# A third down product as seven block products, and LayerNorm statistics of twelve tiles moved to ScalarE

## Chip, cores and metric

One core of a Trainium2 chip. The metric is the device time of one execution in microseconds (us), median of several. Every run is profiled, so each run also has its own span and its own mean granted TensorE clock.

## The reference, cut to what matters

Two layers, each a linear-attention block and a gated bilinear block, on 2048 rows of 1024 bf16 elements. The inner width of the bilinear block is 3584.

```python
x = x + _A_ref(_layernorm(x), A_wqkv, A_wo)               # layer one, attention
x = x + _B_ref(_layernorm(x), B_w_gate, B_w_up, B_w_down) # layer one, bilinear
x = x + _A_ref(_layernorm(x), A_wqkv, A_wo)               # layer two
x = x + _B_ref(_layernorm(x), B_w_gate, B_w_up, B_w_down)
# _B_ref: h = (x @ w_gate) * (x @ w_up);  return h @ w_down
```

## The kernel before

A helper records every operation with what it reads and writes, derives the waits, and emits one instruction stream per engine. So an engine works strictly in the order of the program, and a line of a profile is often a helper's line.

Each bilinear block runs in two passes of 1024 rows: gate/up, then down. A down pass is one two-by-two block multiplication with seven products instead of eight, in the order 1, 2, 6, 7, 4, 5, 3. A *plain* product is 56 matmuls with 512 moving columns. Some products are split once more into seven *block products*, 98 matmuls with 256 columns, 7/8 of the columns. The price of that is VectorE's: eight operand sums S1 to S4 and T1 to T4 of 128x1792 elements, and for product three twelve accumulations of 256 columns out of PSUM.

```python
L2DOWN = {(False, 0): "45", (False, 1): "5", (True, 0): "45", (True, 1): "453"}   # (layer two, pass): products split again
...
def run_l2(q, evac):                                   # a product as seven block products
    ...
    order = ((f, 0), (f, 1), (m2, 0), (m6, 0), (m2, 1), (m6, 1), (m7, 0), (m3, 0), (m7, 1), (m3, 1), (m4, 0), (m4, 1))
    for st_, (fn, r) in enumerate(order):
        fn(r)                                          # one or two block products and their accumulations
        ...
        l2_ops(q, "abcdefghijkm"[st_])                 # operand sums scheduled behind this step
```

The LayerNorm of the next block is spread under the down products (`dticks1`): statistics (two passes of `bn_stats` on VectorE), reciprocal deviation on GpSimd, normalisation, then a DMA transpose. At the start of the kernel there is a second form of the statistics, with two accumulating passes on ScalarE:

```python
def ln_s1(i, dst, r_dst):     # ScalarE: sum of x/D; GpSimd: negate it
    P.add("act", lambda e: e.activation(dst, x_res[:, i, :], AF.Copy, scale=1.0 / D, accum_out=mv[j][:, 0:1]), ...)
def ln_s2(i, j, dst, r_dst):  # ScalarE: sum of (x - mean)^2
    P.add("act", lambda e: e.activation(dst, x_res[:, i, :], AF.Square, bias=mv[j][:, 5:6], scale=1.0, accum_out=mv[j][:, 6:7]), ...)
```

Of the kernel before, what the change touches and what calls it, by code (L numbers as in the profile page):

```python
# [180 lines left out]
def build_kernel(nc, A_x, A_wqkv, A_wo, B_w_gate, B_w_up, B_w_down, out):  # L181
# [21 lines left out]
    ORDER0 = "D3A' P1A P7B' P6A D2B' 51 D4B' D3B' R0 56 D2A P1B T0 P7A 57 P5A W P6B T1 D4A R0 P5B S5+"  # L203
    ORDER1 = "P5A' 47' T0 P7B' D4A' P5B' 11 D3A' R0 51 16 D4B' D2B' P1A 17 T1 56 D3B' P6A P1B 41 R0 57 S5+ S2+ D2A P6B 46 P7A"
    ORDER2 = "11 57' D2B' P7B' 16 T0 P5A' 21 D4B' P1A 17 S2+ D3A' P5B' 26 R0 P6A D2A S5+ 41 27 P1B D3B' 46 51 T1 P7A 47 P6B 56 D4A R0"
    L2DOWN = {(False, 0): "45", (False, 1): "5", (True, 0): "45", (True, 1): "453"}
    DSCHED = {
        "45": {"20": "S1:5 S1:4", "21": "S2:5 S2:4", "22": "S3:5 S4:4", "23": "S4:5", "70": "S3:4 T1:4", "72": "T2:4 T3:4", "73": "T1:5",
               "4d": "T4:4", "4j": "T2:5", "4m": "T3:5", "5d": "T4:5"},
        "5": {"20": "S1:5", "21": "S2:5", "22": "S3:5", "23": "S4:5", "41": "T1:5", "42": "T2:5", "43": "T3:5", "5d": "T4:5"},  # L210
        "453": {"20": "S1:5 S1:4", "21": "S2:5 S2:4", "22": "S3:5 S4:4", "23": "S4:5", "70": "S3:4 T1:4", "71": "S1:3", "72": "T2:4 T3:4", "73": "T1:5",
                "4d": "T4:4", "4f": "S2:3", "4j": "T2:5", "4m": "T3:5", "5d": "T4:5 S4:3", "5h": "T1:3", "5k": "S3:3", "5m": "T2:3", "3d": "T3:3", "3f": "T4:3"},
    }
# [110 lines left out]
    with ExitStack() as es:  # L324
# [13 lines left out]
        def vh(o, n):  # L338
            return ah[:, o // 2: o // 2 + n]
# [156 lines left out]
        class LN:  # L496
# [13 lines left out]
            def dst(self, n):  # L510
# [2 lines left out]
                o = (O_XN + [O_WQ])[n % 3] if self.to == "B" and n < 14 else O_XN[n % 2]  # L513
                return vh(o, D), R(o, D * 2)

            def start(self, i):
                assert i == self.n
                if self.to == "A0" and i in LN_ACT:
                    j = ln_s1(self.order[i], *self.dst(i))
                    self.q_s.append((i, j))  # L520
                else:
                    j = ln_a(self.order[i])
                self.n += 1
                self.q_b.append((i, j))

            def s2(self, upto=NST):
                while self.q_s and self.q_s[0][0] <= upto:
                    i, j = self.q_s.pop(0)
                    ln_s2(self.order[i], j, *self.dst(i))

            def b1_one(self):
                if self.q_b:
# [816 lines left out]
        def layer_B(lnp, nxt, first):  # L1349
# [301 lines left out]
            def down(ps_, ticks, tail):  # L1651
# [30 lines left out]
                def flat(o):  # L1682
                    return vh(o, 1792).rearrange("p (j c) -> p j c", c=256), R(o, 3584)

                def xbuf(i, half=ps_):
                    c0 = 1024 * half + 256 * i
                    return xnT[:, 0:7, c0:c0 + 256], _seg(O_XT, 7, S * 2, c0 * 2, (c0 + 256) * 2)

                tr, ha_ = [flat(O_T + 3584 * i) for i in range(3)], [flat(O_HA + 3584 * i) for i in range(4)]
                sbuf2 = {"4": [xbuf(i) for i in range(3)], "5": tr if "4" in l2d else [xbuf(1 + i) for i in range(3)], "3": [xbuf(i, 1 - ps_) for i in range(3)]}  # L1690
                tbuf2 = {"4": [flat(RE), flat(RE + 3584), flat(O_XN[0])], "5": [xbuf(3) if "4" in l2d else ha_[2], ha_[0], ha_[1]], "3": [ha_[2], ha_[3], xbuf(3, 1 - ps_)]}
                r4 = [(vf(o, 512), R(o, 2048)) for o in (RC, RC + 2048, RB + 28672, RB + 30720)]
                l2w = {}
                for q in l2d:
# [17 lines left out]
                def run_l2(q, evac):  # L1712
                    W = l2w[q]
                    DB, UB = (B_DX, B_DV[:2]) if q == "4" else (B_DV, B_DX[:2] if q == "5" else B_DX[2:])
                    need = {5: ("S1", "T1"), 6: ("S2", "T2"), 7: ("S3", "T3"), 4: ("T4",), 3: ("S4",), 1: (), 2: ()}

                    def mm(i, r, bank, half, start=False):
                        (a, ra), (b, rb) = W["mm"][i]
                        assert all(n in W["done"] for n in need[i]), (q, i, W["done"])
                        P.add("pe", lambda e: [e.matmul(psb(bank)[:, 256 * half:256 * half + 256], a[:, k, 128 * r:128 * r + 128], b[:, k, :],  # L1720
                                                        start=(start and k == 0), stop=(k == 6), skip_group_check=True) for k in range(7)],
                              rd=ra + rb, pwr=[bank])

                    def hf(ap, h):
                        return ap[:, 256 * h:256 * h + 256]

                    def acc(t, h, r, uh, src):
                        d, rd_ = rout[t]
                        sv, rs = src[t]
                        stt(hf(d, h), hf(psb(UB[r]), uh), CD, hf(sv, h), rs, rd_, prd=[UB[r]])  # L1730

                    def put(t, r):
                        P.add("act", lambda e: e.copy(hf(psb(DB[t]), 0), hf(psb(UB[r]), 1)), prd=[UB[r]], pwr=[DB[t]])

                    def put5(t, r):
                        P.add("dve", lambda e: e.tensor_tensor(out=hf(psb(DB[t]), 1), in0=hf(psb(UB[r]), 1), in1=hf(r4[r][0], 0), op=ALU.add),
                              prd=[UB[r]], rd=r4[r][1], pwr=[DB[t]])

                    if q == "3":
                        rin = rout = [(rtmp[4 + t], rr(4 + t)) for t in range(4)]  # L1740
                    else:
                        rin, rout = [xq(1, 0, t) for t in range(4)], r4

                    def first_(r):
                        mm(5, r, UB[r], 0, True)
                        mm(1, r, UB[r], 1)
                        if q == "5":
                            P.add("act", lambda e: e.copy(hf(r4[r][0], 0), hf(psb(UB[r]), 0)), prd=[UB[r]], wr=r4[r][1])
                            put(r, r)
                        else:  # L1750
                            acc(r, 1, r, 0, rin)
                            acc(r + 2, 1, r, 0, rin)
                            acc(r, 0, r, 1, rin)

                    def m6(r):
                        mm(6, r, UB[r], 1)
                        if q == "5":
                            put5(r, r)
                        else:
                            acc(r, 1, r, 1, rout)  # L1760

                    def m7(r):
                        mm(7, r, UB[r], 1)
                        if q == "5":
                            put5(r + 2, r)
                            put(r + 2, r)
                        else:
                            acc(r + 2, 1, r, 1, rout)
                            acc(r + 2, 0, r, 1, rin)

                    def m2(r):
                        mm(2, r, DB[r], 0)

                    def m3(r):
                        mm(3, r, DB[r], 1)
                        evac(r)

                    def m4(r):
                        mm(4, r, DB[r + 2], 0)
                        evac(r + 2)  # L1780
                    f = first_
                    order = ((f, 0), (f, 1), (m2, 0), (m6, 0), (m2, 1), (m6, 1), (m7, 0), (m3, 0), (m7, 1), (m3, 1), (m4, 0), (m4, 1))
                    for st_, (fn, r) in enumerate(order):
                        fn(r)
                        if st_ == 9:
                            ring_issue()
                            ring_issue()
                        l2_ops(q, "abcdefghijkm"[st_])

                tail(0)  # L1790
                for qi, q in enumerate(DPROD):
# [106 lines left out]
            def dticks1(q, t):  # L1898
                if is_last:
                    return  # L1900
                if q != "3":
                    nxt.step_t(1)
                    nxt.b2_one()
                    nxt.b1_one()
                    if t % 2 == 0 and nxt.n < 8:
                        nxt.start(nxt.n)
                if q == "1" and t == 3:
                    for c in (1, 2, 4):
                        tw_load("k", c)
                if q == "7" and t == 3:  # L1910
                    for c in (2, 4):
                        tw_load("q", c)
                if q == "5":
                    s_make(nxt.order, 0)[t]()
                if q == "5" and t == 3:
                    for w in "kq":
                        load_w(w, 0)
                        t, v, c0, base = WSRC[w]
                        dma(t[:, 4:8, 512:1024], v[:, 4:8, c0 + 512:c0 + 1024], _seg(base + 4 * D * 2, 4, D * 2, 1024, 2048), KW[w][1])
                        tw_load(w, 3)  # L1920
                    tw_load("q", 1)
                if q == "3":
                    stash(12 + t)
                    nxt.step_t(1)
                    nxt.b2_one()
                    nxt.b1_one()
                    nxt.start(8 + t)
                    if t == 3:
                        for k in range(4):
                            stash(8 + k)  # L1930
# [77 lines left out]
```

## Time and profile before

| | before |
|---|---|
| median of the first three runs | 1436.43 us (1435.66 to 1438.34) |
| products five and three of layer one's second down pass | 22.78 us (707.96 to 730.74) |
| start of product five to layer two's first gate/up pass | 239.96 us (to 947.92) |
| from there to the end of product five of layer two's first down pass | 230.31 us (to 1178.23) |

The two later marks, and what lies between them, are these lines of the same view (start, duration, what):

```profile
947.92 7.77 PE ps L1385 x36
...
1117.09 7.15 DMA arena<-arena
1124.34 0.55 DVE arena L492
1124.88 0.61 DVE arena L453
...
1160.43 17.75 PE ps L1720 x161
1178.23 10.74 PE ps L1802 x49
```

### The profile page before, as it was taken

How to read it: one execution, taken by the hardware profiler on the slowest of the kernel's cores; microseconds unless marked ns; L12 is line 12 of the kernel's file. 1: busy time of each engine (PE TensorE's matmuls, PEld its weight loads, DVE VectorE, ACT ScalarE, POOL GpSimd, SP SyncE). 2: the span in 40 equal slices, each digit the busy share in tenths (PEclk: the TensorE clock that was granted, in tenths of full speed). 3: DMA queues.
4: the chain of work that ended last, by engine and by line, in shares of the span. 5: the costliest groups of instructions: out<-in, count | busy, mean ns of one | idle time of the engine just before them, and what ended most of it. 6: DMA issues, size and time to landing. Idle time of an engine off the chain costs nothing.

```text
span 1433.9 us, 21771 instructions
## 1 busy us (share of the span) xinstructions
PE 1420.6 (99%) x8107; PEld 786.8 (55%) x8167; DVE 1209.5 (84%) x2370; ACT 688.2 (48%) x1408; POOL 149.9 (10%) x181
## 2 busy tenths in 40 slices
PE   9999999999999999999999999999999999999999
PEld 4444444555546566664544444446766475666547
DVE  6897878999988799988679978778888887888888
ACT  5882355444410266652157813667776004767400
POOL 2203621000010000002000045310000100000000
PEclk9999999999999999999999999999999999999999
DMA  7868978997786777768993266767775976777653
GB/s 227 203 144 234 219 173 199 300 303 266 255 266 211 235 256 255 244 235 300 232 286 96 89 171 165 182 181 254 262 243 194 288 256 226 261 258 259 205 192 120
DMA packets 272586, 320.73 MB, mean 224 GB/s; under 512 B 164064, under 2 KB 215008, under 8 KB 272480
## 3 DMA queue, kind: packets, MB, share of 16 engines
q1 hardware_dynamic: 272480, 319.34, 73.1%
q8 instruction: 64, 1.05, 0.3%
q14 instruction: 42, 0.34, 0.1%
HBM read 236.45 MB, written 73.40 MB: 216 GB/s over the span
## 4 chain that ended last, share of the span: by engine, by line
PE 84%; DVE 8%; ACT 2%; DMA 2%; issue 2%; POOL 1%; SPq 1%; POOLq 0%; DVEq 0%; ACTq 0%
PE ps L1385 28%; PE ps L1466 17%; PE ps L1802 14%; PE ps L1201 8%; PE ps L960 6%; PE ps L1720 5%; PE ps L1303 4%; DVE arena L798 3%; PE ps L928 2%; DMA arena<-arena 1%; DVE arena L453 1%; DVE arena L801 1%; DMA arena<-in_A_wqkv_dram 1%; ACT arena L658 1%; SPq L426 1%
## 5 line engine op out<-in xcount | busy, mean ns | idle before, releaser
L798 DVE TENSOR_TENSOR arena<-arena 128x512 f16<-128x512 f16 (+9 forms) x1019 | 498.8, 517 | 60.1 <-ACT arena L1470 34.2
L1385 PE MATMUL ps<-arena 128*128 128x512 f16 x1888 | 457.0, 379 | 1.0 <-DVE arena L801 0.9
L801 DVE SCALAR_TENSOR_TENSOR arena<-ps,arena 128x512 f16<-128x512 f32 (+3 forms) x545 | 353.8, 663 | 68.5 <-PE ps L1802 28.4
L1466 PE MATMUL ps<-arena 128*128 128x256 f16 x2184 | 287.5, 273 | 1.0 <-DVE ps L1479 1.0
L1385 PEld LDWEIGHTS ps<-arena 128*128 128x128 f16 (+1 forms) x1888 | 182.9, 98 | 163.4 <-ACT ps L1414 3.8
L1466 PEld LDWEIGHTS ps<-arena 128*128 128x128 f16 (+1 forms) x2184 | 212.2, 98 | 91.5 <-ACT arena L1470 6.9
L1802 PE MATMUL ps<-arena 128*128 128x512 bf16 (+1 forms) x1102 | 242.6, 379 | 0.9
L1802 PEld LDWEIGHTS ps<-arena 128*128 128x128 f16 x1120 | 109.5, 98 | 130.4 <-DVE arena L798 0.4
L1390 ACT ACTIVATE arena<-ps 128x512 f32<-128x512 f32 x224 | 133.8, 597 | 76.4 <-PE ps L1385 61.6
L1470 ACT ACTIVATE arena<-ps 128x256 f32<-128x256 f32 x351 | 125.1, 384 | 26.9 <-PE ps L1466 22.0
L960 PE MATMUL ps<-arena 128*128 128x512 f16 (+1 forms) x606 | 134.1, 379 | 1.0 <-ACT arena L967 0.4
L1201 PE MATMUL ps<-arena 128*128 128x512 bf16 x498 | 114.7, 379 | 0.7
L1303 PE MATMUL ps<-arena 128*128 128x512 bf16 x502 | 110.3, 379 | 0.5
L456 POOL TENSOR_SCALAR arena<-arena 128x1 f32<-128x1 f32 x59 | 20.8, 353 | 806.8 <-DVE arena L455 806.8
L1476 ACT COPY ps<-ps 128x256 f32<-128x256 f32 x182 | 66.3, 364 | 74.6 <-DVE arena L801 28.3
L960 PEld LDWEIGHTS ps<-arena 128*128 128x128 f16 x616 | 59.5, 98 | 74.7 <-ACT arena L967 5.8
L1414 ACT COPY ps<-ps 128x512 f32<-128x512 f32 x112 | 65.4, 584 | 64.3 <-PE ps L1385 52.1
L1062 POOL TENSOR_TENSOR arena<-arena 128x1024 f16<-128x1024 f32 x32 | 78.2, 2445 | 154.6 <-DVE arena L1060 146.3
L1720 PE MATMUL ps<-arena 128*128 128x256 f16 (+1 forms) x784 | 86.8, 273 | 0.7 <-DVE arena L801 0.5
L453 DVE BATCH_NORM_STATS2 arena<-arena 128x6 f32<-128x512 bf16 x118 | 81.3, 689 | 5.4 <-DMA arena<-in_A_x_dram 3.3
L1479 DVE TENSOR_TENSOR ps<-ps,arena 128x256 f32<-128x256 f32 x182 | 76.6, 427 | 10.5 <-PE ps L1466 9.5
L1303 PEld LDWEIGHTS ps<-arena 128*128 128x128 f16 x512 | 50.1, 98 | 60.4
(70 smaller groups left out, 939.8 us busy)
## 6 DMA issues: line engine op xcount, KB each, us to landing
arena<-w_scratch SPq DMA_DIRECT2D x84, 896.0 KB, 4.6
arena<-t_scratch SPq DMA_DIRECT2D x32, 896.0 KB, 6.1
arena<-in_B_w_down_dram SPq DMA_DIRECT2D x24, 896.0 KB, 5.7
arena<-sp_scratch SPq DMA_DIRECT2D x26, 768.0 KB, 4.2
w_scratch<-arena SPq DMA_DIRECT2D x28, 512.0 KB, 6.3
arena<-w_scratch SPq DMA_DIRECT2D x28, 384.0 KB, 4.8
x_scratch<-arena SPq DMA_DIRECT2D x40, 256.0 KB, 7.7
arena<-x_scratch SPq DMA_DIRECT2D x40, 256.0 KB, 5.6
```

The lines of the kernel that those rows point to most:

```text
L453: P.add("dve", (lambda h: lambda e: e.bn_stats(st[j][:, 6 * h:6 * h + 6], x_res[:, i, (D // 2) * h:(D // 2) * (h + 1)]))(h), rd=r_x(i, (D ...
L798: P.add("dve", lambda e: e.tensor_tensor(out=out, in0=a, in1=b, op=op), rd=rd, wr=wr, prd=prd)
L801: P.add("dve", lambda e: e.scalar_tensor_tensor(out=out, in0=a, scalar=sc, in1=b, op0=ALU.mult, op1=op1), rd=rd, wr=wr, prd=prd)
L960: P.add("pe", lambda e: [e.matmul(psb(bank), a[0][:, k, :], b[0][:, k, :], start=(q in (1, 5) and k == 0), stop=(k == 3), skip_group_check ...
L1201: return [e.matmul(psb(bank), xrt[t][:, jj * 128:(jj + 1) * 128], pk[:, h, t, :], start=(t == tok[0]), stop=(t == tok[NST - 1])) for t in ts]
L1303: return [e.matmul(psb(bank), xnT[:, g, i * 128:(i + 1) * 128], wp[:, g, dh * 512:(dh + 1) * 512], start=(dh == 0 and g == 0), stop=(g == ...
L1385: P.add("pe", lambda e: [e.matmul(psb(bank), w[:, k, :], x[:, k, :], start=(start and k == 0), stop=(k == 3), skip_group_check=True) for k ...
L1390: P.add("act", lambda e: e.activation(t, psb(bank), AF.Copy, scale=SG), prd=[bank], wr=r)
L1466: P.add("pe", lambda e: [e.matmul(psb(bank)[:, 256 * half:256 * half + 256], w[:, k, :], xx[:, k, :], start=(start and k == 0), stop=(k == ...
L1470: P.add("act", lambda e: e.activation(d, src, AF.Copy, scale=sc), prd=[xk], wr=rd_)
L1720: P.add("pe", lambda e: [e.matmul(psb(bank)[:, 256 * half:256 * half + 256], a[:, k, 128 * r:128 * r + 128], b[:, k, :], start=(start and ...
L1802: P.add("pe", lambda e: [e.matmul(psb(bank), hv[:, 7 * hf + k, t * 128:(t + 1) * 128], w[:, k, :], start=(q in "15" and hf == 0 and k == 0 ...
```

## The change

Its intent: product three of that pass as seven block products too, for fewer TensorE cycles, with VectorE's room for the sums made by moving the statistics of twelve of sixteen tiles to ScalarE, which is nearly idle there. The core of the diff (cut: a throwaway buffer for the passes' outputs, operand buffers for product three):

```diff
-    L2DOWN = {(False, 0): "45", (False, 1): "5", ...}
+    L2DOWN = {(False, 0): "45", (False, 1): "53", ...}
-        "5": {..., "5d": "T4:5"},
+        "53": {..., "40": "S1:3", ..., "5b": "S2:3", "5d": "T4:5",
+               "5f": "S3:3", "5i": "T1:3", "5m": "T2:3", "3b": "T3:3", "3d": "S4:3", "3f": "T4:3"},
@@ class LN
-                if self.to == "A0" and i in LN_ACT:
-                    j = ln_s1(self.order[i], *self.dst(i))
+                if self.to == "A0" and i in LN_ACT or self.to == "A" and i < 12:
+                    j = ln_s1(self.order[i], *self.junk(i))
@@ run_l2
                         l2_ops(q, "abcdefghijkm"[st_])
+                        ticks(q + "s", st_)
@@ dticks1
+                if q == "3s":
+                    if t < 8:
+                        nxt.s2() if t % 2 else nxt.start(8 + t // 2)
+                    elif t == 8:
+                        nxt.b1_one()
+                        nxt.b2_one()
+                    return
+                if q == "5s" and t < 4:
+                    s_make(nxt.order, 0)[t]()
...
                 if q == "3":
                     stash(12 + t)
-                    nxt.step_t(1)
-                    nxt.b2_one()
-                    nxt.b1_one()
-                    nxt.start(8 + t)
```

## The prediction

> **What bounds the kernel now.** I read the page from its top: engines, slices, chain; then the chain and the timeline around the changed stretch, the waits in it, and the end of the run, where the kernel already does a third product as seven blocks.
>
> ```profile
> PE 1420.6 (99%) x8107; PEld 786.8 (55%) x8167; DVE 1209.5 (84%) x2370; ACT 688.2 (48%) x1408; POOL 149.9 (10%) x181
> PEclk9999999999999999999999999999999999999999
> PE 84%; DVE 8%; ACT 2%; DMA 2%; issue 2%; POOL 1%; SPq 1%; POOLq 0%; DVEq 0%; ACTq 0%
> ```
> TensorE is busy or nearly so everywhere at full clock and carries 84% of the chain. So only two things pay: fewer TensorE cycles, and no new wait in front of it. VectorE has 8% of the chain; where, matters below.
>
> ```profile
> 663.55 44.41 PE ps L1802 x205
> 707.96 10.70 PE ps L1720 x98
> 718.71 10.74 PE ps L1802 x49
> ...
> 730.74 10.36 PE ps L960 x48
> ```
> This is the chain in order of time (start, duration, what). L1802 is a plain down product, L1720 one done as seven blocks, L960 the q/k projections of layer two. The fifth product (blocks) takes 718.71 - 707.96 = 10.75 us, the third (plain, and last) 730.74 - 718.71 = 12.03 us. The chain runs through TensorE alone: there is no stall to remove here.
>
> ```profile
> 712.92 1.08 DVE L798 TENSOR_TENSOR arena<-arena 128x1792 f16<-128x1792 f16 x1
> 715.34 0.36 ACT L1733 COPY ps<-ps 128x256 f32<-128x256 f32 x1 [3.64 <-DVE ps L1736]
> 722.32 1.41 DVE L453 BATCH_NORM_STATS2 arena<-arena 128x6 f32<-128x512 bf16 x2
> 725.58 1.24 ACT L489 ACTIVATE arena<-arena 128x1024 f16<-128x1024 bf16 x1 [8.19 <-DVE arena L483]
> ```
> The timeline of the same stretch: VectorE has one operand sum of the fifth product left, then evacuations and one LayerNorm statistic per evacuation; ScalarE is nearly idle. In the stretch 707.96 to 730.74 VectorE is busy 6.89 + 8.17 = 15.06 of 22.78 us, ScalarE 2.01 + 2.48.
>
> ```profile
> 1414.07 2.08 DVE L798 TENSOR_TENSOR arena<-arena 128x1792 f16<-128x1792 f16 x2
> 1422.52 2.07 DVE L801 SCALAR_TENSOR_TENSOR arena<-ps,arena 128x256 f32<-128x256 f32 x6
> 1426.30 4.48 PEld L1720 LDWEIGHTS ps<-arena 128*128 128x128 f16 x42 [0.27 <-DVE arena L798]
> ```
> The timeline of the last down pass, where products five and three are both blocks. A sum starts 1.0 us after the one before it, a 256-wide accumulation 2.07/6 = 0.345 us after. Such a third product has waited for a sum there, but only 0.27 us.
>
> ```profile
> 35.78 1.05 ACT L468 ACTIVATE arena<-arena 128x1024 f16<-128x1024 bf16 x1
> 37.64 1.15 ACT L475 ACTIVATE arena<-arena 128x1024 f16<-128x1024 bf16 x1 [0.72 <-POOL arena L470]
> 38.70 0.19 ACT L475 ACTIVATION_READ_ACCUMULATOR arena<-arena 128x1 f32 x1
> 38.79 0.57 ACT L649 ACTIVATE arena<-ps 128x512 bf16<-128x512 f32 x1
> ```
> ScalarE's timeline at the start of the kernel, where five tiles get their statistics this way already: one tile, from its first pass to the next instruction, takes 38.79 - 35.78 = 3.01 us, 0.72 of it waiting for the negated mean from GpSimd.
>
> **What the Trainium skill says.** "TensorE: Matmul & The Clock Gate", section Back-to-back issue gap, gives N/2.4 + 2.5 ns for an isolated warm gap: 215.8 ns for 512 columns, 109.2 for 256. The trace agrees: 12.03/56 = 214.8 and 10.75/98 = 109.7 ns. The same section's sustained 131 ns for 512 columns does not occur here. So halving the columns halves the price, and 7/8 of the columns is really worth nearly 1/8. "VectorE: DVE Perf Modes", section The perf-mode tier table, caps a two-tensor operation at the double rate in bf16 SBUF and at the single rate with PSUM; here 1792 SBUF elements take 1.08 us and 256 with a PSUM operand already 0.42. "ScalarE: Activation LUTs", section What ACT_TABLE_LOAD costs, gives an ACTIVATE with immediate scale and bias as 186 + 0.833 N ns, and some 93 ns more per pointer operand: 1.04 and 1.13 us at 1024 elements. The passes above took 1.05 and 1.15; the accumulator's read (0.19) is not in that figure.
>
> **The change part by part.**
> TensorE: 56 matmuls of 512 columns go (12.03 us), 98 of 256 columns come (10.75 us, measured on product five): -1.28 us, all on the path.
>
> VectorE, off: 12 tiles x (2 x 0.69 + 0.21) = 19.1 us of statistics; eight of them lie under products one to seven, where TensorE waits for nobody (55 us of unbroken chain), and are worth nothing there. VectorE, on: 8 sums x 1.0 = 8.0 us and 12 accumulations x 0.345 = 4.1 us, nearly all between 708 and 730, where four tiles' 6.4 us go. I ran this queue by hand in issue order. In product five (start 707.96, block 0.768 us): last evacuation and sum of before until 709.6, then S2, T4, S3, T1, four smaller sums moved here (0.35 each), four PSUM additions and four evacuations. The additions that later blocks wait for end at 712.9, 714.6, 716.0 and 717.0, and with ScalarE's copies behind the last two 716.4 and 717.4; the blocks want them at 714.1, 715.6, 717.1 and 717.9. No stall, least slack 0.5 us. T1 of product three ends at 718.0, before its first block at 718.7. T2 ends at 720.8, six accumulations at 722.8, T3 at 723.8, S4 at 725.2, T4 at 726.5; the blocks that use T2, T3, S4, T4 want them at 722.5, 724.8, 725.5, 727.8. Least slack 0.3 us, so I allow 0.15 us for a missed one.
>
> ScalarE: 12 tiles x 3.0 us = 36 us of added occupancy with its waits, in a stretch where it is idle; the first eight are harmless. The last four are in one queue: from 717.4, after the last copy of product five, 4 x 3.01 = 12.0 us to 729.4, then a normalising pass of 1.24 to 730.7. Layer two starts at about 729.5; its first ScalarE copy can start at 730.5 and is wanted 1.2 us before its third block at 731.2, less 0.57 for the copy: 0.1 us of stall.
>
> Layer two: one pass per tile of the normalisation slips from the third product into the projections, and there it runs on VectorE instead of ScalarE.
>
> ```profile
> 743.21 1.13 ACT arena L489
> ...
> 756.78 0.46 DVE arena L492
> ```
> The chain in the projections: at 743 it runs through ScalarE's normalising pass, and TensorE's weight loads then wait 0.66 us where 0.16 is usual; that pass moves to VectorE, which has room there: about -0.4 us. From 754 to 787 the chain runs through VectorE (31.90 of 33.00 us busy), and by the order of the queue exactly one more normalising pass falls into this stretch: +0.45 us (its length on the chain).
>
> Sum: -1.28 + 0.15 + 0.1 - 0.4 + 0.45 = -0.98 us.
>
> **The rivals.** (a) VectorE becomes the bound of products five and three. For: 0.3 us of slack in my count, and a wait of 0.27 in the last pass; here two more sums fall inside. Against: that pass lacks nothing else. One full sum too many costs 1.0 us in each product: the time would be 1436.4 to 1437.5. (b) ScalarE's queue of four tiles delays the seam. For: 12.0 us of passes in 12.0 us of time; a late start by 1 us is a late copy by 1 us. Then -0.2, 1436.2. (c) Relief counts: 19 us off VectorE against 12 on shortens something. For: 84% busy. Against: the statistics lie where TensorE has no wait; only the two tiles at 728.5 and 731.5 touch the projections, and VectorE idles after them. With the gain at 743 full and no loss at 760 it would be -1.7, 1434.7. (d) Weight loads: DMA engines are 99% busy between 695 and 745, and an earlier start could meet a late load. Against: the matrices of the first block were issued at 717 to 719.5 and land in 7 to 9 us.
>
> **Range and chances.** 1436.43 - 0.98 = 1435.4 us. The three runs of before span 1435.66 to 1438.34, so their noise is as large as the effect, and lies above the median; the rivals span 1434.7 to 1437.5. Range 1434.0 to 1437.2. The whole saving on TensorE is 0.09% of the time, and even rival (a) is far below 2%: within 2% 0.98, 0.01 each for the others.
>
> **What would show it.** Third product as 98 matmuls in 10.7 to 11.0 us; no TensorE wait over 0.3 us in products five and three; ScalarE's passes of the last four tiles ending near 729.5; the pass at 743 gone from ScalarE and the wait behind it down to 0.2 us; two more normalising passes on VectorE after the seam; start of the g products (820.7 before) about 1 us earlier. Wrong if the seam is later than 730.4, if projections take over 90.5 us, or if anything outside 640 to 825 us moves by over 0.5 us.

## More of the kernel before

Where a gate/up pass ends in layer two, eight tiles of the residual (2 MB) are loaded again, and only then, with the first down product, come the DMA transposes of the last LayerNorm tiles:

```python
# end of gateup(), tail part 3
for t in range(8 if l2 and not jit else 0):
    dma(x_res[:, i, :], xscr[i * 128:(i + 1) * 128, :], r_x(i), KX[i], ...)
...
def dticks0(q, t):                       # under the products of the first down pass
    if q in "12" and not lnp.done():
        lnp.flush_step()                 # transpose one tile, normalise the next, statistics of the one after
```

The times come from the chain that ended last, in order of time; the prediction shows its lines up to 730.

## The result

The changed kernel: 1436.49 us median (1436.04 to 1436.98, 4 runs), against 1436.05 (1435.22 to 1438.34, 4 runs) of the kernel before on the same chip. Ratio 1.0001, 95% interval 0.9983 to 1.0018: the same. Ratios are the mean time of one kernel's fast runs over that of the other's of the same rounds, so not quite the ratio of the medians quoted.

The chain after, with the lines that answer to those of before (helper lines have moved by one to five: L1724 is a product in blocks, L1807 a plain one, L964 the projections, L1389 gate/up, L493 a normalisation on VectorE):

```profile
707.55 4.60 PE ps L1724 x42
...
712.61 1.33 DVE arena L802 x2
...
728.40 0.61 DVE arena L805
729.01 10.78 PE ps L964 x49
...
946.31 7.77 PE ps L1389 x36
...
1115.45 9.14 DMA arena<-arena
1124.69 0.55 DVE arena L493
...
1160.80 17.75 PE ps L1724 x161
1178.60 10.74 PE ps L1807 x49
```

From 712 to 729 us this chain runs through VectorE, where that of before ran through TensorE alone. TensorE has no gap there all the same (its timeline shows the 196 matmuls of the two products in 21.56 us without a break), and in the second profile of this kernel the chain stays on TensorE for 21.40 us. So the two engines come out level: VectorE has next to no slack left in these products.

Products five and three now take 729.01 - 707.55 = 21.46 us, 1.32 less. From the start of product five to layer two's first gate/up pass it is 238.76 us, 1.20 less. The gain is there, and at 946 us it is complete: the kernel is 1.61 us ahead, 0.41 of it from differences before product five. But by 1178.60 it is 0.37 us *behind*. The next stretch takes 232.29 us instead of 230.31. It holds gate/up and down work that the change does not touch.

What happened there stands in the timelines around 1115 us. Before:

```profile
1112.66 4.39 SPq L426 DMA_DIRECT2D arena<-x_scratch  x8
1117.09 9.05 SPq L572 DMA_TRANSPOSE arena<-arena  x3
1124.34 0.55 DVE L492 TENSOR_SCALAR arena<-arena 128x1024 f16<-128x1024 bf16 x1 [4.54 <-DMA arena<-arena]
```

After:

```profile
1111.06 4.35 SPq L427 DMA_DIRECT2D arena<-x_scratch  x8
1115.45 11.05 SPq L576 DMA_TRANSPOSE arena<-arena  x3
1124.69 0.55 DVE L493 TENSOR_SCALAR arena<-arena 128x1024 f16<-128x1024 bf16 x1 [6.49 <-DMA arena<-arena]
```

The bracket is the idle time of the engine before that instruction and what ended it. VectorE's next normalisation overwrites a buffer that a transpose still reads, so its whole in-order queue waits. The transposes were issued 1.64 us earlier (1115.45 for 1117.09), but VectorE got on 0.35 us later: the wait grew from 4.54 to 6.49 us. (The 9.05 and 11.05 us of the SPq rows are the time in which SyncE's queue issued all three transposes. VectorE waits for the first of them alone: by the chains it landed 7.15 us after its issue before, and 9.14 us after the change.)

The DMA view of 1115 to 1127 us shows a difference. Its second line is the rate in 40 slices of 0.3 us. Before:

```profile
GB/s 287 406 406 434 416 331 389 403 389 430 396 376 403 437 389 382 423 389 341 369 410 369 339 249 124 229 301 278 103 10 271 152 0 0 0 0 5 195 215 207
q14 instruction: 1, 0.01, 0.2%
```

After:

```profile
GB/s 365 389 362 382 403 410 396 410 410 396 403 417 396 389 403 369 387 298 278 168 12 0 7 7 7 15 182 307 273 132 10 230 195 0 0 0 0 0 160 214
q8 instruction: 1, 0.02, 0.5%
q14 instruction: 1, 0.01, 0.2%
```

In the middle of the transposes the rate drops to about zero for six slices, 1.8 us. And there is one transfer on queue 8 that is not there before. That queue has 64 transfers of 16 KB in the whole execution, and TensorE has 8150 + 8209 = 16359 matmul and weight-load instructions: 255.6 for each. So I take it for TensorE's instruction fetch, one for every 256 instructions; the runs below that add TensorE instructions bear this out, since these transfers move with them. In the trace's list of transfers this one starts at 1120.9 us, and 21 packets beside it take up to 2.41 us, where 99% of such packets in this stretch of the kernel before take under 0.1. The change adds 42 matmuls and as many weight loads before this point, so every later fetch comes 84 instructions sooner: the neighbouring fetches of the kernel before were at 1104.6 and 1132.7, on both sides of its transposes.

That gave three theories: A, the fetch falls among the transposes in this program and delays them; B, the wait differs from run to run; C, the transposes are held by a fixed limit of the DMA queues.

### The profile page after: what moved, and what is told of

It is laid out like the page before. It is cut to its first block, busy times and chain, and to the rows that moved or that the text cites. A ratio compares the mean times of both kernels' runs of the same rounds, so it can differ in the third digit from the quotient of the medians.

```text
span 1434.3 us, 21907 instructions
## 1 busy us (share of the span) xinstructions
PE 1418.5 (99%) x8150; PEld 790.2 (55%) x8209; DVE 1205.3 (84%) x2354; ACT 713.4 (50%) x1454; POOL 153.9 (11%) x193
## 3 DMA queue, kind: packets, MB, share of 16 engines
q8 instruction: 64, 1.05, 0.3%
## 4 chain that ended last, share of the span: by engine, by line
PE 86%; DVE 8%; ACT 2%; issue 2%; DMA 1%; POOL 1%; SPq 0%; POOLq 0%; DVEq 0%
PE ps L1389 28%; PE ps L1470 17%; PE ps L1807 13%; PE ps L1205 8%; PE ps L964 8%; PE ps L1307 6%; PE ps L1724 5%; DVE arena L802 4%; PE ps L932 2%; DVE arena L805 1%; DVE arena L454 1%; DMA arena<-arena 1%; DMA arena<-in_A_wqkv_dram 1%; ACT arena L662 1%; PE ps L1231 1%
## 5 line engine op out<-in xcount | busy, mean ns | idle before, releaser
L802 DVE TENSOR_TENSOR arena<-arena 128x512 f16<-128x512 f16 (+7 forms) x1027 | 507.5, 522 | 59.0 <-ACT arena L1474 34.1
L1389 PE MATMUL ps<-arena 128*128 128x512 f16 x1888 | 457.0, 379 | 0.1
L805 DVE SCALAR_TENSOR_TENSOR arena<-ps,arena 128x512 f16<-128x512 f32 (+3 forms) x557 | 358.2, 659 | 76.0 <-PE ps L1807 36.8
L1389 PEld LDWEIGHTS ps<-arena 128*128 128x128 f16 (+1 forms) x1888 | 183.0, 98 | 162.5 <-ACT ps L1418 3.8
L1807 PE MATMUL ps<-arena 128*128 128x512 bf16 (+1 forms) x1048 | 230.9, 379 | 2.5 <-DVE arena L802 1.6
L1807 PEld LDWEIGHTS ps<-arena 128*128 128x128 f16 x1064 | 103.9, 98 | 126.0 <-DVE arena L802 2.1
L964 PE MATMUL ps<-arena 128*128 128x512 f16 (+1 forms) x605 | 134.0, 379 | 1.2 <-ACT arena L971 0.6
L964 PEld LDWEIGHTS ps<-arena 128*128 128x128 f16 x616 | 59.4, 98 | 74.7 <-ACT arena L971 5.8
L1724 PE MATMUL ps<-arena 128*128 128x256 f16 (+1 forms) x882 | 97.5, 273 | 0.7 <-DVE arena L805 0.5
L1724 PEld LDWEIGHTS ps<-arena 128*128 128x128 f16 x882 | 86.0, 98 | 12.4 <-DVE arena L805 0.8
L1307 PEld LDWEIGHTS ps<-arena 128*128 128x128 f16 x512 | 50.1, 98 | 60.4
L1752 ACT COPY arena<-ps 128x256 f32<-128x256 f32 x8 | 3.0, 372 | 158.5 <-PE ps L1724 158.5
```

Source lines behind the costliest of these rows:

```text
L802: P.add("dve", lambda e: e.tensor_tensor(out=out, in0=a, in1=b, op=op), rd=rd, wr=wr, prd=prd)
L805: P.add("dve", lambda e: e.scalar_tensor_tensor(out=out, in0=a, scalar=sc, in1=b, op0=ALU.mult, op1=op1), rd=rd, wr=wr, prd=prd)
L964: P.add("pe", lambda e: [e.matmul(psb(bank), a[0][:, k, :], b[0][:, k, :], start=(q in (1, 5) and k == 0), stop=(k == 3), skip_group_check ...
L1307: return [e.matmul(psb(bank), xnT[:, g, i * 128:(i + 1) * 128], wp[:, g, dh * 512:(dh + 1) * 512], start=(dh == 0 and g == 0), stop=(g == ...
L1389: P.add("pe", lambda e: [e.matmul(psb(bank), w[:, k, :], x[:, k, :], start=(start and k == 0), stop=(k == 3), skip_group_check=True) for k ...
L1724: P.add("pe", lambda e: [e.matmul(psb(bank)[:, 256 * half:256 * half + 256], a[:, k, 128 * r:128 * r + 128], b[:, k, :], start=(start and ...
```

## The experiments

Each profile was read with the same ruler, from three marks of the chain and the wait of VectorE's normalisation:

| run | five to gate/up | gate/up to end of five, layer two | VectorE's wait | fetch after issue of the transposes |
|---|---|---|---|---|
| before | 239.96 | 230.31 | 4.54 | none among them |
| before_again | 239.97 | 230.26 | 4.52 | none |
| before_pad84 | 239.98 | 230.26 | 4.52 | 7.44 us |
| before_pad100 | 239.99 | 230.49 | 4.70 | 6.52 us |
| before_pad118 | 239.96 | 230.52 | 4.79 | 7.44 us |
| after | 238.76 | 232.29 | 6.49 | 5.47 us |
| after_again | 238.75 | 231.84 | 6.10 | 5.98 us |
| after_pad172 | 238.76 | 230.19 | 4.45 | none |
| blocks_only | 244.42 | 231.78 | 5.97 | 5.53 us |
| stats_only | 241.21 | 230.55 | 4.75 | none |
| after_reload_late | 238.75 | 229.55 | 0 | (transposes spread out) |
| before_reload_late | 239.99 | 229.59 | 0 | (spread out) |
| after_ln_early | 238.74 | 232.88 | (no transposes there) | |
| before_ln_early | 239.97 | 232.88 | (none there) | |

Two things are to be seen. Wherever VectorE had that wait, the second stretch less the wait is 225.73 to 225.81 us: between 4.45 and 6.49 us, each further microsecond of the wait is one of the kernel. The first part of it is free: without any wait (the two `reload_late` runs) the stretch is 229.6 us and not 225.8, so some 3.8 us of waiting cost nothing. And every unaltered first stretch is 239.96 to 239.99 before and 238.74 to 238.76 after: the change's own gain is 1.20 to 1.25 us in each profile.

**The changed kernel again.** No edit.

> The changed kernel once more, nothing edited. What is to be explained: in its profile the seam from the third down product to the projections comes 1.3 us earlier, counted from the start of product five, and the kernel is 1.6 us ahead at 946 us, but 0.4 us behind at 1160, because in layer two's first down pass the DMA transposes of three tiles take 11.05 us from issue to landing where they took 9.05, and VectorE's in-order queue waits for them 6.5 us instead of 4.5. Theory A (one position of TensorE's instruction fetch): the fetch at 1120.9 falls among these transposes in every run of this program, so this profile shows the fetch within 1 us of 1120.9, packets over 2 us beside it and a wait of 6.2 to 6.8 us again, and the ratio to before is 1.000. Theory B (chance): the wait differs from run to run, so it may be 4.5 us here. Theory C (a fixed limit of the DMA queues): no slow packets, but the transposes land at 1124 to 1125 us again.

Measured: 1437.49 us median, ratio 1.0007 (0.9995 to 1.0020). Fetch at 1121.1 us, wait 6.10 us; 24 packets of the transposes beside it take over 1 us, up to 1.42. The collision is there again, a little milder than theory A said (its packets over 2 us are missing). A second fetch has a part in the picture: the transfer on queue 14 (8 KB, also of the kind "instruction", so presumably another engine's) falls into the pause here and in `blocks_only` and takes 1.77 and 1.86 us. Alone it does no harm: in the six profiles without a TensorE fetch in the first 7 us after the issue it lies 5.7 to 6.2 us after it as well, takes 0.31 to 0.40 us, and VectorE's wait is 4.45 to 4.79. Nor is it needed: in the first profile of the changed kernel it came at 7.9 us, after the pause. The three of the five runs over 1437 probably had something else, see the next run; their own profiles were not kept.

**The kernel before again.** No edit.

> The kernel before once more, nothing edited, as the null. Theories A and C: wait of VectorE for the transposes 4.3 to 4.8 us, no fetch between 1117 and 1124. Theory B: it may be anything from 4 to 7 us. Ratio 1.000 with an interval of about 0.001 either way.

Measured: 1437.16 us, ratio 1.0006 (0.9993 to 1.0018): the null is as far from 1 as the run above. The wait is 4.52 us, the fetches at 1106.7 and 1133.8, as A and C said. What made this run long is the start. The stretches of 4 us at the start, of this run (columns: stretch, its length, busy time of each engine with its instructions, granted clock, DMA share, GB/s):

```profile
8.00:12.00 4.00, 1.73 (x9) 0.65 (x8) 2.23 (x5) 1.08 (x2) 0.79 (x2) 1.00 1.09 363
12.00:16.00 4.00, 4.00 (x19) 1.77 (x18) 2.34 (x6) 1.95 (x3) 0.79 (x2) 0.62 1.09 355
```

and of the first profile of the kernel before:

```profile
8.00:12.00 4.00, 2.56 (x13) 1.00 (x12) 2.75 (x7) 1.09 (x2) 0.80 (x2) 1.00 1.08 366
12.00:16.00 4.00, 3.71 (x24) 1.74 (x23) 2.70 (x7) 2.24 (x4) 0.86 (x2) 1.00 1.09 355
```

TensorE was idle longer while it waited for weights between 8 and 12 us, and its clock was cut to 0.62 for the next 4 us. (The idle time alone does not bring the cut: in the first profile of the changed kernel TensorE was busy for only 1.81 us between 8 and 12 us, and its clock stayed at 1.00. Why it was cut here is open.) Product five then starts at 709.46 instead of 707.96. Runs over 1437 us often show a mean clock of 0.999 instead of 1.000. So below I also give the mean of the runs at 1.000. For the kernel before, eight of nine such runs on this chip: 1435.75 us. For the changed kernel, six in the first job, whose chip is not on record, and this one: 1436.34 (the two on this chip: 1436.03).

**The changed kernel with its fetches moved.**

```diff
                     for s, v in ws[1:]:
                         eng.wait_ge(s, v)
+                    if e == "pe" and 270 <= op.pos < 442:      # 172 groups of the first gate/up pass
+                        eng.wait_ge(esem["pool"], 1)           # long since satisfied
```

> The changed kernel with 172 already satisfied waits on TensorE, one before each of 172 groups of the first gate/up pass, where TensorE's array is the bound. They are instructions, so TensorE's fetches of 256 instructions come 172 later, which with the change's own 84 makes 256: the fetches after 707 us fall where they fall in the kernel before. Theory A: fetch near 1103 and 1131, none among the transposes, wait of VectorE 4.3 to 4.8 us, time 1.2 to 2.0 us under the changed kernel (ratio to before about 0.999). Theory B and C: wait as in the other run of the changed kernel, time the same or a little longer for the waits added.

Measured: 1434.49 us (1434.26 to 1436.73), ratio 0.9994 (0.9981 to 1.0006); at clock 1.000 four runs, mean 1434.62. The fetches lie at 1107.7 and 1134.2, no packet of the transposes takes over 0.6 us, and the timeline has the wait of before:

```profile
1115.85 8.99 SPq L578 DMA_TRANSPOSE arena<-arena  x3
1123.04 0.55 DVE L495 TENSOR_SCALAR arena<-arena 128x1024 f16<-128x1024 bf16 x1 [4.45 <-DMA arena<-arena]
```

172 useless instructions make the changed kernel 1.7 us faster by these means, 1.4 if only the runs on the same chip are taken, and it is then 1.1 us under the kernel before. That is theory A's number; theory C has no way to it, and B only by luck. The ratios' intervals are too wide to carry this alone; the stretches do: 230.19 us against 232.29 and 231.84.

**The kernel before with its fetches moved onto the transposes,** in three attempts. The edit is the same with 84, 118 and 100 groups.

> The kernel before with 84 such waits in the same place: its fetches after 707 us then fall where the changed kernel has them, near 1122 us. Theory A: the fetch meets the transposes, VectorE's wait grows from 4.5 to about 6.5 us, time 1.5 to 2.0 us over the kernel before. Theories B and C: nothing systematic, within 0.5 us of before.

> The kernel before with 118 satisfied waits instead of 84: with 84 the fetch came at 1124.0, just after the transposes had landed at 1123.9, and VectorE's wait stayed at 4.52 us, so that run did not test what it was made for. 118 move it some 3.5 us earlier, to about 1120.5, into the middle. Theory A (fetch among the transposes delays them): packets over 1.7 us there, wait 6 to 6.6 us, time 1.3 to 2.0 us over the kernel before in runs of granted clock 1.000. Theories B (chance) and C (fixed limit): wait 4.5 us, no slow packets.

> The kernel before with 100 satisfied waits on TensorE: with 84 and with 118 the fetch came 7.44 us after the issue of the transposes, when they had landed, and hit nothing. Between the two counts of instructions, 16 more than 84 are 1.7 us: the fetch at 5.7 us, among the 256-byte packets (4.5 to 7.3 us). If it falls there, theory A wants packets over 1.5 us, a wait of 6.0 to 6.6 us and 1.3 to 2.0 us more than the kernel before; if it falls at 7.4 again, the wait is 4.5 us and nothing is lost. A fetch at 5 to 6.5 us with a wait of 4.5 us would break theory A.

Measured: 84: 1435.81 us, ratio 1.0004 (0.9990 to 1.0018), fetch 7.44 us after the issue of the transposes, when the awaited one had landed (after 7.22 us): a miss. 118: 1437.61 us, ratio 1.0009 (0.9997 to 1.0022), fetch at 7.44 us again and not 3.5 us sooner, 0.1 us before the awaited transpose landed, wait 4.79. 100: 1436.28 us, ratio 1.0004 (0.9990 to 1.0017), fetch at 6.52 us, which itself took 1.58 us; 19 packets of the transposes took over 1 us, up to 1.48; wait 4.70. I had written that a fetch at 5 to 6.5 us with a wait of 4.5 would break theory A. This one is on the edge. In the undisturbed traces most of the awaited 256-byte packets have gone through by 6.5 us and a gap follows (in the kernel before no transpose packet ends between 7.4 and 9.0 us); here the pause fell on that gap, from 7.5 to 8.9 us, so it delayed little. I could not place a fetch as finely as I had thought, and so the loss was not produced in the kernel before. Also open: four runs of the one with 118 at clock 1.000 have a mean of 1437.49 us, 1.3 over the nine of the kernel before on that chip (1436.18), and the one profile read, a run at 0.999, shows only 0.25 of that.

**The normalisation moved out of the down pass,** in both kernels.

```diff
             def ticks0(u):
+                if not first and u % 4 == 0 and u >= 4 and not lnp.done():
+                    lnp.flush_step()
```

> The changed kernel with the normalisation of the last tiles of layer two's second LayerNorm, and their transposes, spread over the first gate/up pass of layer two, 140 us before they are used, instead of under the first down product. Theory A: with no transposes behind the eight reloads, VectorE has nothing to wait for, and the fetch has nothing to hit. TensorE took 50.5 us there where 203 matmuls of 214.8 ns and the 0.9 us before them make 44.5: up to 6 us come back, less what two statistics and two passes cost in a gate/up pass where VectorE is over 90% busy (0 to 1.5 us). Time 1431 to 1433 us. If the loss is not in that wait (theory C: the reloads of 2 MB set the pace), under 1 us comes back.

> The same edit of the kernel before. Here 48.6 us stand against 44.5, so up to 4 us come back: 1432 to 1434 us. What the change itself is worth, with the collision out of both, is the difference to the same edit of the changed kernel: theory A says 1.0 to 1.3 us, as the seam shows; a theory that block product and statistics gain nothing says 0.

Measured: 1437.12 us, ratio 1.0012 (0.9998 to 1.0025), and 1438.89, ratio 1.0019 (1.0007 to 1.0032). Both are slower by their medians, where a gain was expected: a clear miss. The down pass did run without a stall, 66.25 us from 1113.40 to 1179.65. But gate/up took 1113.40 - 946.77 = 166.63 us instead of 163.30. VectorE, busy for 85% of that pass and not the over 90% of my expectation, had 4.0 us more to do there (143.39 for 139.36), and TensorE's weight loads waited four times for its accumulations, 4.0 us together, which they did not do before. And my figure of "up to 6 us" was wrong. I had taken the chain's first block-product piece (1160.43) for the start of product four, but the chain had only been on VectorE before it. TensorE really lost 67.03 - 66.25 = 0.78 us in that pass before (an expectation below has 66.97 for 67.03) and 68.99 - 66.25 = 2.74 after. The first stretch shows the change's gain once more, 239.97 against 238.74.

**The reloads behind the transposes,** in both kernels.

```diff
-                    for t in range(8 if l2 and not jit else 0):
+                    for t in range(8 if l2 and not jit and (first or ps_) else 0):
@@ evac of the down pass
                         ticks(q, t)
                         l2_ops(q, t)
+                        if q in "12" and not first and ps_ == 0:
+                            i = 4 * "12".index(q) + t
+                            dma(x_res[:, i, :], xscr[i * 128:(i + 1) * 128, :], r_x(i), KX[i], ...)
```

> The changed kernel with the eight reloads of the residual (2 MB) issued one by one under the first two products, each behind its transposition, instead of all ahead of the transposes. If the transposes wait in the DMA queues behind the reloads, VectorE's wait falls from 6.5 to under 2 us and the time by 3 to 5 us, fetch or no fetch. If the transposes are slow by themselves, the wait stays over 4 us.

> The kernel before with the reloads issued behind the transposes, as in the run of the changed kernel that was the fastest so far. There the wait of VectorE vanished and TensorE went through that pass without a stall: from its first product to the end of the fifth 66.25 us, against 66.97 in the kernel before and 68.99 in the changed kernel. So here 0.7 us are to be had: 1435.0 us at granted clock 1.000. The changed kernel with this edit took 1433.6 to 1434.8 at that clock; the difference of 1.0 to 1.3 us is what the change is worth where nothing takes it back. If the change were worth nothing, this run would be as fast.

Measured: the changed kernel 1434.72 us (1433.64 to 1435.24), ratio to before 0.9988 (0.9975 to 1.0000), at clock 1.000 three runs, mean 1434.05. The kernel before 1434.97, ratio 0.9993 (0.9981 to 1.0006), mean of four at 1.000 1435.10. The waits on DMA are gone from VectorE, the transposes are issued one by one and each takes 1.2 to 1.3 us at the queue. The timeline of the changed kernel with this edit:

```profile
1112.46 1.24 SPq L576 DMA_TRANSPOSE arena<-arena  x1
1115.98 1.24 SPq L576 DMA_TRANSPOSE arena<-arena  x1
1120.64 1.25 SPq L576 DMA_TRANSPOSE arena<-arena  x1
```

and its chain in the same pass, which stays on TensorE:

```profile
1112.05 43.81 PE ps L1807 x203
1155.86 9.17 PE ps L1724 x84
```

So it was the reloads ahead of them that made the transposes late, but only in part by the DMA queues. In the kernel before the first transpose now lands 5.87 us sooner (1118.37 for 1124.24). 4.57 us of this come from its issue (1112.52 for 1117.09), because SyncE's in-order queue no longer spends 4.4 us on issuing the eight reloads first, and 1.30 us from the time between issue and landing (5.85 for 7.15 us). In the changed kernel a fetch falls into the same stretch here too (1119.85 us), but between two transposes, of which one landed at 1119.81 and the next was issued at 1120.64; so this run does not show what a fetch among them would cost here. The gain is that of the stall, 2.7 us on the changed kernel's stretch, 0.7 on the other's; the 3 to 5 us that I had expected suffered from the same wrong count as above. Between the two kernels with this edit lie 1.05 us at clock 1.000, and 469.58 - 468.30 = 1.28 us from the start of product five to 1177. (They ran on two chips, so the stretches say more.) This is the fastest version: 0.12% under the kernel before in the ratio, with an interval that just touches 1.

**The block products alone.**

```diff
-                if self.to == "A0" and i in LN_ACT or self.to == "A" and i < 12:
+                if self.to == "A0" and i in LN_ACT:
```

> The changed kernel with the seven block products of product three, but with all LayerNorm statistics on VectorE as before (four of them now between the block products). Theory of the change (VectorE has no room for both): in the changed kernel VectorE works almost without a gap from 712 to 729 us and its last sum comes just in time, so four statistics of 1.6 us in that queue, 6.5 us, push the blocks back: products five and three take 24 to 27.5 us instead of 21.4, and the time is 3 to 6 us over the changed kernel. Rival (the ScalarE part is not needed): 21.4 to 22.0 us, time within 0.6 us of the changed kernel.

Measured: 1442.50 us, ratio 1.0043 (1.0030 to 1.0055). TensorE's timeline:

```profile
728.80 6.42 PE L1724 MATMUL ps<-arena 128*128 128x256 f16 x42 [1.92 <-DVE arena L805]
735.28 1.67 PE L964 MATMUL ps<-arena 128*128 128x512 bf16 x7
738.25 10.10 PE L964 MATMUL ps<-arena 128*128 128x512 f16 x45 [1.29 <-ACT ps L967]
```

Products five and three take 735.28 - 709.43 = 25.85 us by this timeline, against 729.00 - 707.39 = 21.61 in the changed kernel by the same view. The blocks wait for accumulations that stand behind statistics in VectorE's queue, and the projections then wait for a normalising pass that came late. The rival is out: without the ScalarE part, the block products lose 5.7 us on the first stretch (244.42 for 238.76).

**The statistics alone.** Product three plain again; the last four tiles' passes start at its evacuations.

```diff
-    L2DOWN = {..., (False, 1): "53", ...}
+    L2DOWN = {..., (False, 1): "5", ...}
                 if q == "3":
                     stash(12 + t)
+                    nxt.s2()
+                    nxt.start(8 + t)
+                    if t == 3:
+                        nxt.s2()
+                        nxt.b1_one()
+                        nxt.b2_one()
```

> The changed kernel with the statistics on ScalarE but product three plain again. Theory: 12 tiles' statistics off VectorE (19 us of work) save nothing by themselves, because TensorE waits for nobody there: products five and three 22.8 us as before, TensorE's instruction count as in the kernel before, so no fetch among the transposes (VectorE's wait 4.5 us), time within 0.5 us of the kernel before at granted clock 1.000. Rival (relief counts): 0.5 to 1.5 us faster.

Measured: 1437.02 us, ratio 1.0009 (0.9997 to 1.0022). Wait 4.75 us, as expected. Products five and three take 730.44 - 707.65 = 22.79 us by TensorE's timeline, exactly as before by the same view (730.58 - 707.79). So 19 us off VectorE bring nothing in these products; the total can't decide it. That the first stretch is 1.25 us *longer* than before is of my edit's making: it puts the first normalisation behind the last evacuation, and the projections wait for it, in TensorE's timeline:

```profile
730.44 1.89 PE L965 MATMUL ps<-arena 128*128 128x512 bf16 x8
733.26 15.06 PE L965 MATMUL ps<-arena 128*128 128x512 f16 x68 [0.94 <-ACT ps L968]
```

## Why the prediction was right or wrong

The range and the "within 2%" held, but that says little: the range, 1434.0 to 1437.2, holds the kernel before as well, and that the measured time fell into it is in part luck, since a loss of 2.0 us that the prediction had not foreseen met a gain of 1.2. The centre, 1435.4, was 1.1 us under the measured median. The mechanism of the gain was right (0.98 us predicted, 1.20 measured, and the difference is mostly two allowances that were not needed), and something that the prediction excluded took the gain back.

*TensorE, -1.28 us.* Right: 22.78 to 21.46 us, 1.32 less, with no stall of TensorE in its timeline, so the allowance of 0.15 was not needed.

*VectorE's queue, done by hand.* Right. Shifted by the 0.41 us that product five started earlier, T1, T2, S4 and T4 should end at 717.6, 720.4, 724.8 and 726.1; the timeline has 717.53, 720.32, 724.76 and 726.09. Two of its lines, after:

```profile
708.20 3.09 DVE L802 TENSOR_TENSOR arena<-arena 128x1792 f16<-128x1792 f16 x5
719.24 1.08 DVE L802 TENSOR_TENSOR arena<-arena 128x1792 f16<-128x1792 bf16 x1
```

VectorE is busy 20.44 of these 21.46 us. Rival (a) did not come about, but only just: the chain already runs through VectorE there, and the run without the ScalarE part loses 5.7 us.

*ScalarE's queue.* Right: the last pass was to end at 729.0 after the same shift.

```profile
728.70 0.19 ACT L476 ACTIVATION_READ_ACCUMULATOR arena<-arena 128x1 f32 x1
728.79 1.23 ACT L490 ACTIVATE arena<-arena 128x1024 f16<-128x1024 bf16 x1
729.93 0.57 ACT L967 COPY ps<-ps 128x512 f32<-128x512 f32 x1
```

It ended at 728.89, and the first copy of the projections found the engine just free. Rival (b) is out.

*The projections, -0.4 and +0.45 us, and 0.1 at the seam.* Right: from the seam to gate/up 217.30 us for 217.18, 0.12 more where 0.15 was predicted. The chain no longer passes ScalarE at 743, and the wait there is 0.16 us. The two terms can be read apart from the timelines of the weight loads, if the same loads are counted from the seam (730.74 before, 729.01 after). Before, and after:

```profile
764.48 5.82 PEld L960 LDWEIGHTS ps<-arena 128*128 128x128 f16 x28 [0.22 <-ACT arena L967]
770.53 5.81 PEld L960 LDWEIGHTS ps<-arena 128*128 128x128 f16 x28 [0.23 <-ACT arena L967]
```

```profile
762.40 4.96 PEld L964 LDWEIGHTS ps<-arena 128*128 128x128 f16 x24 [0.22 <-ACT arena L971]
768.91 5.73 PEld L964 LDWEIGHTS ps<-arena 128*128 128x128 f16 x28 [0.68 <-ACT arena L971]
```

The first of them comes at 33.74 us before and at 33.39 after, 0.35 us sooner; the second at 39.79 and 39.90, so 0.46 us were lost between them. Both terms were right. Of the 0.1 us at the seam nothing is seen: the first two ScalarE copies behind the q/k products start 0.90 and 2.63 us after it before, 0.92 and 2.62 us after the change. (The prediction's own figures, a copy that can start at 730.5 and must by 731.2 - 0.57 = 730.6, leave 0.1 us to spare and none to lose.)

*Rival (c), relief counts.* Out: it wanted 1.7 us off the time, but the first stretch shortens by 1.20 us, TensorE's own 1.32 less 0.12; and with the statistics alone products five and three take as long as before. That run can't speak for the projections, where its edit made a wait of its own. *Rival (d), late weights.* Out: no wait for weights at the seam.

*The step that failed* is one that the prediction used without weighing it: that nothing moves outside 640 to 825 us. It named the sign ("if anything outside 640 to 825 us moves by over 0.5 us"), and that sign appeared: +1.98 us between 946 and 1179 in the profiled run, +1.53 in the next. What stands in its place is VectorE's wait for the first of three DMA transposes in layer two's first down pass. In each of three profiles in which TensorE's instruction fetch began 5.5 to 6.0 us after their issue, that wait was 5.97 to 6.49 us, and in the seven others that had it 4.45 to 4.79. Moving the fetches by instructions that do nothing gave the time back in the changed kernel (wait 4.45 us). So it is shown that the longer wait took the gain back. That the fetch causes the pause in the transposes is strongly supported, but it rests on these coincidences and on that one run; the opposite test in the kernel before did not hit. The profile of before held half of the warning: a chain that runs through a DMA transpose and then 36 us through VectorE. I saw the 8% of VectorE in the chain and looked for it only beside the change.

## What to carry to other kernels

A local gain is only worth what the rest of the program lets through: follow the chain from the change to the end, and look for every place where an engine waits for a transfer with no slack behind it. Added instructions move every later instruction fetch of their engine, and here an effect of 0.1% was masked when one fell among transfers that an engine waited for; compare by stretches between marks of the chain, not by totals alone, and a kernel with a few harmless instructions more is a cheap control. Transfers that someone waits for belong ahead of bulk transfers that are needed later, in the queue that issues them too: here eight reloads took 4.4 us to issue.

## What the Trainium skill lacked or had wrong

- "Runtime: NRT & Kernel Launch", section Instruction fetch mechanics, has the fetch in 16 KiB blocks of 256 instructions (the runs agree: 16359 instructions, 64 transfers) and calls its cost mostly hidden. It lacks what a fetch can cost the kernel's own transfers: beside one, packets of DMA transposes took up to 2.41 us, and the stretch with them was 1.5 to 2.0 us longer (that the fetch is the cause is strongly supported, not proved).
- "DMA: Bandwidth & Descriptors", section DMA Transpose (X-bar), gives no figure for transposes issued behind bulk loads or beside a fetch. Here those behind 2 MB of loads kept VectorE waiting for 4.5 to 4.8 us, and 6.0 to 6.5 with a fetch among them; with the loads issued later there was no wait.
- "TensorE: Matmul & The Clock Gate", section Back-to-back issue gap: its sustained 131 ns for 512 columns does not occur in this kernel; the isolated gap that it gives beside it is what the runs show (214.8 ns).
- No page gives the cost of a ScalarE pass with an accumulator: the read of it is an instruction of its own of 0.19 us, and a tile's two passes with GpSimd's step between them took 3.0 us.
